# Queries and keys of eighteen couples loaded in 32-row quarters and turned by VectorE's block transpose

## The chip, the core and the metric

The kernel runs on one core of a Trainium2 chip. Its engines work from queues of their own and meet through semaphores: TensorE (PE in the profile; its weight loads are PEld), VectorE (DVE), ScalarE (ACT), GpSimd (POOL) and SyncE (SP), which here only issues DMAs. The metric is the device time of one execution in microseconds (us); the kernel before has a median of 1347.96 us over three runs.

## The reference

All data is float32. Attention over 8 batches of 12 heads with 448 rows of 64 is followed by a feed-forward block over the 3584 rows that come out.

```python
def rmsnorm(x, g):
    rms = np.sqrt(np.mean(x * x, axis=-1, keepdims=True) + 1e-06)
    return x / rms * g
q_n, k_n = (rmsnorm(q, g_q), rmsnorm(k, g_k))
scores = (1.0 / np.sqrt(64)) * np.matmul(q_n, k_n.transpose(0, 1, 3, 2))
scores = scores - np.max(scores, axis=-1, keepdims=True)
attn = np.exp(scores)
attn = attn / (np.sum(attn, axis=-1, keepdims=True) + 1e-09)
attn_out = np.matmul(attn, v)
# (B, H, S, D) -> (B * S, H * D), then
h = x @ w_in                          # 3584 x 768 by 768 x 2048
g = h * (1.0 / (1.0 + np.exp(-h)))
return g @ w_out                      # 2048 x 768
```

## The kernel before, in words

**Stages.** The 96 heads are worked off in 24 couples of four heads, `c` = 0 to 23 (two pairs, index `i`, of two heads, index `h`); three couples make a batch, and six (`GROUP`) two batches. Couples 0 to 5 run with little else beside them. From couple 6 on, the first product of the feed-forward block for the two batches before is worked in between, as a filler. After couple 23 come the first product of the last two batches and then the whole second product ("quads"). Both products save multiplications by sums of quarters (classes `Seven` and `deep`), whose additions are on VectorE and GpSimd. Everything in this stretch is recorded in an order that is written out by hand: each engine executes its instructions in just the order in which the loop `visit(c)`, `between(c)` issues them.

**A couple.** `visit(c)` makes scores of key tile by key tile on TensorE (`scores`, L595), exponentials on ScalarE (L600), and the weighted sums of `v` (`weigh`, L632). Scores are made transposed, with keys on partitions, so 1/rms of a key can be the scale of the exponential: `norm.column` is the `rms` operand at L600. A query's 1/rms has to be on its row before it is turned. Keys beyond 384 of the 448 are a tile of their own (`LEFT`). In the visit after, `weigh` finishes the couple and `divide` (L690) multiplies the two sums `av` by reciprocals. `turn` (L608) writes one column of a bank from ScalarE where the order of the two halves of `weigh` changes, which makes TensorE wait for the products so far.

**Between couples.** `transpose_q(c + 1)` turns the rows of q on TensorE, 8 transposes into PSUM (L558), and ScalarE copies them to `qT` (L562); `transpose_k` does the same for k with 7 (L576) and the copy applies the gains (L578). `sum_up` sums the exponentials on TensorE (L666), VectorE takes reciprocals (L675), and `spread` sends them to the partitions where `divide` needs them, by four and then two DMAs (L681, L683) on SyncE. `fill` issues the filler's products (L767) up to a share of columns: from couple 6 on about 14 steps (28 instructions) in each of its two calls. While it does so it deals out the work in `others` evenly, and the work in `prompt` one piece at the start and one after each third step. The results of the products leave their PSUM banks (`mm`, two of them) by VectorE (L725) or ScalarE (L775, L785), GpSimd adds parts (L787, L788), ScalarE applies SiLU in place (L905), and SyncE saves the hidden rows to DRAM (L800).

**Norms.** `normalise(c)` squares rows on ScalarE (L401), reduces them on VectorE (L402), forms mean + eps there (L426), takes the power -1/2 on GpSimd (L430), and, for q alone, multiplies the rows by it on GpSimd (L445). For q the columns are 16 of 112 partitions, for k 14 of 128.

**Loads.** All go through SyncE in program order: for one couple from 6 on q by 2 DMAs (L245), k by 4 (L252, L256), v by 1 (L261) and the last keys' v by 3 (L266, L269). Row `4p + j` of q lies on partition `p`, so the rows of `out` come out in that order, and `store` writes four interleaved pieces. From couple 6 q has one place (`q0`), k two. Until couple 8 W_in's pieces are loaded as well (L75), and until couple 10 they are rounded (L90, L91, L113, L116, L120, L124), and sums of them are made on VectorE (`sum_w_in`).

Of the kernel before, what the change touches and what calls it, by code (L numbers as in the profile page):

```python
# [30 lines left out]
class Shapes:  # L31
    def __init__(self, q, w_in):
# [19 lines left out]
        assert self.NW == self.NPAIR and self.B % 2 == 0  # L52

# [127 lines left out]
def kernel(  # L181
# [32 lines left out]
    ring = const.tile([P, nq + 2 * z.NK + nv + 2 * (4 * D + 2 * D)], F32, name="rows")  # L214
    place, at = {}, 0
    for name, size in (
        ("q0", nq), ("k0", z.NK), ("k1", z.NK), ("v", nv),
        ("vlast0", 4 * D), ("vlast1", 4 * D), ("vleft0", 2 * D), ("vleft1", 2 * D),
    ):
        place[name] = ring[:, ds(at, size)]  # L220
        at += size
# [10 lines left out]
    def load_q(c, t, by_head, steps=1):  # L232


        b, cp = divmod(c, z.NPAIR // 2)
        rows = q[b, ts(cp, 4)]
        if by_head:
            for i in range(steps):
                n = 4 // steps
                dst = t[0:R, ts(i, nq // steps)].rearrange("p (n j d) -> p n (j d)", n=n, j=J)  # L240
                nc.sync.dma_start(dst, rows[ts(i, n)].rearrange("n (p j) d -> p n (j d)", j=J))
            return
        for i in range(2):
            dst = t[0:R, ts(i, nq // 2)].rearrange("p (j h d) -> p j h d", j=J, h=2)
            nc.sync.dma_start(dst, rows[ts(i, 2)].rearrange("h (p j) d -> p j h d", j=J))  # L245

    def load_k(c):
        t = place[f"k{c % 2}"]
        main, left = keys_of(k, c)
# [7 lines left out]

    def load_v(c):
        main, _ = keys_of(v, c)
# [3 lines left out]
    def load_v_rest(c):  # L263
        main, left = keys_of(v, c)
# [22 lines left out]
    rms = [const.tile([P, 32], F32, name=f"rms{i}") for i in range(2)]  # L287
    spare = const.tile([P, 3 * J * D], F32, name="squares")
# [17 lines left out]
    with tc.manual_schedule(), tc.tile_pool(  # L306
        name="ps_first", bufs=1, space=bass.MemoryType.PSUM
    ) as ps_first:
        load_q(0, first_q, True, 2)
        load_k(0)  # L310
        load_q(1, second_q, True)
# [48 lines left out]
    def arm():  # L360
# [9 lines left out]
                second_q=second_q,  # L370
# [77 lines left out]
def store(nc, out, z, column, o, m0, *queues):  # L448
# [3 lines left out]
    while at < o.shape[0]:  # L452
        b, c = divmod(column + at, z.S)
        j, p = divmod(c, z.R)
# [8 lines left out]
def bounded(  # L463
# [10 lines left out]
    NC, loads, place, norm, spare, ones, first = (  # L474
        own[name] for name in ("NC", "loads", "place", "norm", "spare", "ones", "first")
# [52 lines left out]
    def load_q(c):  # L528

        if 0 < c < GROUP:  # L530
            loads["q"](c, raw_of(c), True)
        elif GROUP <= c < NC:
            loads["q"](c, q_of(c), False)
# [15 lines left out]
    def transpose_q(c):  # L549
# [13 lines left out]
        if c == GROUP - 2:  # L563
            load_q(GROUP)
        elif c >= GROUP:
            load_q(c + 1)

    def transpose_k(c):
# [10 lines left out]
        if c + 2 < NC:  # L579
            loads["k"](c + 2)  # L580

# [4 lines left out]
    def scores(c, j, i=None):  # L586
# [12 lines left out]
        for h in range(2):  # L599
            nc.scalar.activation(  # L600
                eleft[:, h] if j == LEFT else weights(c, j)[:, i, h], two[:, h, 0:S], AF.Exp,
                scale=norm.column(c, i, h, j),
            )

    def turn(step):

        if step != weighed["step"]:
            nc.scalar.copy(banks[1][:, S : S + 1], minus_half)  # L608
# [85 lines left out]
    def normalise(c):  # L694


        if c >= NC:
            return []

        def piece(name, i):  # L700
            t = scratch[i if c < GROUP + 2 else 0]
            source = raw_of(c) if c < GROUP else q_of(c)
            if name == "q":
                norm.squares_q(c, source, t, i)
            else:
                norm.squares_k(c, place[f"k{c % 2}"], t, i)
            if name == "q" and c < GROUP:
                norm.root(c, name, i)
                norm.scale(c, source, q_of(c), i, nc.gpsimd)
                if i == 1 and c + 2 < GROUP:  # L710
                    load_q(c + 2)
            elif i == 1:
                norm.root(c, name)
                if name == "q":
                    for m in range(2):
                        norm.scale(c, source, q_of(c), m, nc.gpsimd)
# [400 lines left out]
    def save_out(q, i, j):  # L1117
        for t in range(2):
            store(
                nc, out, z, (4 * q + 2 * (i - 1) + t) * P, results[i, j][t], (j - 1) * z.HALF,  # L1120
                nc.gpsimd if q == QUADS - 1 and i == 2 else nc.sync,
# [476 lines left out]
```

## Time and profile before

| | |
|---|---|
| runs | 1347.61, 1347.96, 1348.33 us; median 1347.96 |
| profiled execution | 1347.41 us, of which the span of the profile is 1345.6 |
| busy in the span | PE 1312.5 us (98%), DVE 915.4 (68%), ACT 519.6 (39%), POOL 346.3 (26%) |
| TensorE clock granted | 0.999 of full speed |
| DMA, from 160 to 733 us | 16 engines busy for 0.32, 89 GB/s |
| PE busy, 0 to 113 us | 102.5 of 113 |
| PE busy, 113 to 160 us | 42.9 of 47 |
| PE busy, 160 to 733 us | 563.4 of 573 |
| PE busy, 733 to 1346 us | 603.7 of 613 |

The stretch from 113 us is the hand-over from couple 5 to couples 6 and 7, that from 160 us holds couples 7 to 23, and that from 733 us what follows. An engine's busy time tells nothing of what waits for what; for that there is the chain that ended last, which follows each step back to what released it, and, behind a row of the timeline, the idle time before it with its releaser. A row `L430 POOL ... x23 | 64.2, 2791 | 143.5 <-DVE rms L426` reads: 23 instructions of line 430 on GpSimd, 64.2 us busy in all, 2791 ns each on the mean, 143.5 us of idle time of that engine just before them, ended most often by VectorE's line 426. `SPq` is the time in which SyncE's sequencer issues a DMA.

### The profile page before, as it was taken

To read this page: it belongs to the slowest core of one execution; us is meant where nothing else is said; L and a number is where in the kernel's file an instruction comes from. 1 tells how busy PE (TensorE), PEld (TensorE's weight loads), DVE (VectorE), ACT (ScalarE), POOL (GpSimd) and SP (SyncE) were. 2 spreads that over 40 slices of the span, in tenths; PEclk is the share of its full clock that TensorE was granted. 3 is DMA by queue.
4 is the path that set the end of the run, shared out by engine and by line. 5 is a ranking of instruction groups with operands and counts; after the bars stand their busy time and mean duration, and the time that the engine had idled before them with its cause. 6 is when DMAs were issued, how large, how long until landed. Compare 5 with 4: busy or idle time off the path is not lost.

```text
span 1345.6 us, 19745 instructions
## 1 busy us (share of the span) xinstructions
PE 1312.5 (98%) x7345; PEld 848.1 (63%) x7345; DVE 915.4 (68%) x1593; ACT 519.6 (39%) x932; POOL 346.3 (26%) x241
## 2 busy tenths in 40 slices
PE   8989999999999999999999999999999999999997
PEld 4333444444444444444444455557999999999997
DVE  5787776785645444644544586789878787878785
ACT  7866565655445455545544244320000000101000
POOL 6766534343133233332231044420000000000001
PEclk9999999999999999999999999999999999999999
DMA  8564437223223223222311257422323232322311
GB/s 234 161 166 113 124 89 203 76 80 106 74 81 80 79 78 101 74 72 80 106 52 38 100 175 262 150 98 68 104 75 99 75 100 79 99 92 88 115 59 39
DMA packets 175421, 139.41 MB, mean 104 GB/s; under 512 B 104052, under 2 KB 159284, under 8 KB 175316
## 3 DMA queue, kind: packets, MB, share of 16 engines
q1 hardware_dynamic: 174640, 137.08, 34.4%
q8 instruction: 60, 0.98, 0.3%
q0 software_dynamic: 352, 0.79, 0.2%
q14 instruction: 45, 0.37, 0.1%
q10 hardware_dynamic: 324, 0.20, 0.1%
HBM read 88.47 MB, written 41.29 MB: 96 GB/s over the span
## 4 chain that ended last, share of the span: by engine, by line
PE 83%; DVE 5%; ACT 5%; DMA 3%; issue 2%; SPq 1%; POOL 0%; ACTq 0%; DVEq 0%; POOLq 0%
PE mm L767 25%; PE alone L1074 22%; PE mm L1074 7%; PE av L632 7%; PE alone L767 7%; PE sc L595 7%; PE alone L1111 2%; DVE work L675 1%; PE sc L558 1%; DMA work<-work 1%; PE sc L576 1%; DMA hidden<-stage 1%; PE sc L666 1%; ACT work L600 1%; ACT L1358 1%
## 5 line engine op out<-in xcount | busy, mean ns | idle before, releaser
L767 PE MATMUL mm<-x,W 128*128 128x448 f32 x636 | 253.9, 543 | 3.1 <-DVE stage L725 1.2
L600 ACT ACTIVATE work<-sc,rms 128x448 f32<-128x448 f32 x324 | 184.9, 634 | 76.8 <-PE sc L595 63.9
L430 POOL TENSOR_TENSOR rms<-rms,minus_half 128x14 f32<-128x14 f32 (+4 forms) x55 | 140.9, 2563 | 236.5 <-DVE rms L426 187.0
L767 PEld LDWEIGHTS mm<-x,W 128*128 128x128 f32 x636 | 117.8, 190 | 125.0 <-issue 107.3
L767 PE MATMUL mm<-sums_x,W 128*128 128x448 f32 x456 | 183.0, 542 | 2.0 <-DVE parts L725 2.0
L632 PE MATMUL av<-work,rows 64*64 64x448 f32 x1296 | 156.1, 543 | 12.2 <-ACT av L608 9.6
L595 PE MATMUL sc<-work 64*64 64x448 f32 x1344 | 165.4, 542 | 1.1 <-ACT work L600 1.1
L646 DVE TENSOR_TENSOR work<-work 128x896 f32<-128x896 f32 (+1 forms) x114 | 124.5, 1125 | 49.2 <-PE av L632 48.6
L767 PEld LDWEIGHTS mm<-sums_x,W 128*128 128x128 f32 x456 | 85.3, 190 | 87.7 <-issue 80.8
L457 POOL DMA_DIRECT2D out_dram<-x x4 | 2.2, 565 | 442.7 <-DVE x L725 442.7
L632 PEld LDWEIGHTS av<-work,rows 64*64 64x64 f32 x1296 | 59.3, 132 | 86.3 <-issue 34.2
L595 PEld LDWEIGHTS sc<-work 64*64 64x64 f32 x1344 | 56.0, 132 | 75.8 <-issue 25.9
L402 DVE TENSOR_REDUCE rms<-squares 112x8 f32<-112x512 f32 (+1 forms) x80 | 52.2, 652 | 65.1 <-ACT squares L401 61.2
L1074 PE MATMUL alone<-W,rows 128*128 128x192 f32 x488 | 92.1, 326 | 0.0
L787 POOL TENSOR_TENSOR parts<-parts,stage 128x448 f32<-128x448 f32 x31 | 42.1, 1357 | 161.7 <-DVE parts L725 161.7
L1074 PEld LDWEIGHTS alone<-W,rows 128*128 128x128 f32 x488 | 81.5, 190 | 0.0
L1074 PE MATMUL alone<-W,work 128*128 128x192 f32 x382 | 72.2, 326 | 0.0
L905 ACT ACTIVATE stage<-stage 128x896 f32<-128x896 f32 x63 | 57.3, 945 | 26.1 <-DVE stage L725 25.4
L1084 ACT COPY squares<-alone 128x192 f32<-128x192 f32 x34 | 10.8, 317 | 137.5 <-PE alone L1074 79.0
L1074 PEld LDWEIGHTS alone<-W,work 128*128 128x128 f32 x382 | 63.8, 190 | 0.0
L401 ACT ACTIVATE squares<-rows 128x512 f32<-128x512 f32 (+1 forms) x74 | 44.8, 605 | 47.7 <-DVE rms L402 46.0
L675 DVE RECIPROCAL work<-sc 128x224 f32<-128x224 f32 x36 | 55.6, 1547 | 11.1 <-PE sc L666 11.1
(249 smaller groups left out, 2122.2 us busy)
## 6 DMA issues: line engine op xcount, KB each, us to landing
hidden<-stage SPq DMA_DIRECT2D x63, 448.0 KB, 2.7
work<-hidden SPq DMA_DIRECT2D x21, 1024.0 KB, 5.0
rows<-in_moe_w_out_dram SPq DMA_DIRECT2D x32, 384.0 KB, 3.4
W<-in_moe_w_in_dram SPq DMA_DIRECT2D x22, 512.0 KB, 5.1
rows<-in_k_dram SPq DMA_DIRECT2D x48, 192.0 KB, 3.1
work<-work SPq DMA_DIRECT2D x144, 56.0 KB, 1.9
rows<-in_q_dram SPq DMA_DIRECT2D x36, 224.0 KB, 3.5
x<-hidden SPq DMA_DIRECT2D x7, 1024.0 KB, 5.7
```

The lines of the kernel that those rows point to most:

```text
L401: nc.scalar.activation(t, rows, AF.Square)
L402: nc.vector.tensor_reduce(out=out, in_=t.rearrange("p (n d) -> p n d", n=n), axis=AX.X, op=ALU.add)
L430: nc.gpsimd.tensor_tensor(out=t, in0=t, in1=half, op=ALU.pow)
L595: nc.tensor.matmul(two[ds(half * D, D), h, 0:S], keys[rows, ts(half, D)], qT[rows, pair, :], start=True, stop=True,)
L600: nc.scalar.activation(eleft[:, h] if j == LEFT else weights(c, j)[:, i, h], two[:, h, 0:S], AF.Exp, scale=norm.column(c, i, h, j),)
L632: nc.tensor.matmul(sums[i][ds(h * D, D), :], v, w, start=(j == 0 and step == 1), stop=(j == LEFT - 1 and step == 1),)
L646: nc.vector.tensor_tensor(out=total, in0=total, in1=more, op=ALU.add)
L675: nc.vector.reciprocal(out=r[0][:, rows], in_=t[:, rows])
L767: nc.tensor.matmul(t, self.left(name, s), self.right(name, s), start=s == ends[0], stop=s == ends[1])
L787: nc.gpsimd.tensor_tensor(out=u2, in0=u2, in1=p5, op=ALU.add)
L905: nc.scalar.activation(t, t, AF.Silu)
L1074: nc.tensor.matmul(t, x[:, i], y, start=i == ORDER[0], stop=i == ORDER[-1])
```

## The change

For couples 6 to 23, q and k are loaded so that the 32x32 blocks of the tile are turned in place. A head's 448 rows are 14 blocks of 32 rows; the two halves of its 64 features go to two quarters of 32 partitions each, for two heads 128 partitions. In a row of the tile lie 14 blocks x 2 pairs of 32 values: 128 x 896. VectorE's block transpose then gives `qT` or `kT` at once, in SBUF, without PSUM and without the copy for q (`flip`); ScalarE still applies the gains, now in place.

Since a row's features lie in two quarters, each quarter gives half a sum of squares (`sum_squares`: one Square and one reduction for 128x896). One matmul with a matrix that has ones at its own and at the partner's place adds the halves (`pair_up` makes that matrix of `ident` once, after the last use as an identity); VectorE forms mean + eps of the result, and GpSimd takes the power and multiplies the rows, for k now too (`scale`). So the exponential gets the scale 1.0 in place of k's column. `scale` for couple `c + 2` stands at the end of `between(c)`; for couples 6 and 7 it has earlier or later places of its own.

Rows and keys are in plain order from couple 6 on, so v is loaded in plain order (4 DMAs for the first tiles, 4 for the last ones), and `store` writes rows of `out` from batch 2 on in one piece for each batch that a tile touches. The place `q0` has moved to the end of the ring and the squares share the end of it that the new q does not use. `turn(1)` uses VectorE in couples from 6 on. The four sums of one set of W_in's weights are dealt out in one fill in place of two. Couples 0 to 5 are as before.

```diff
@@ Shapes @@
+        self.Q = 32
+        assert 2 * self.S == self.NK and 4 * self.Q == self.P and self.D == 2 * self.Q
+
+    def quarters(self):
+
+        return [
+            (h, half, ds((2 * h + half) * self.Q, self.Q)) for h in range(2) for half in range(2)
+        ]
@@ loads @@
+    def load_quarters(rows, t):
+
+        rows = rows.rearrange("n (a p) d -> n p a d", p=z.Q)
+        for i in range(2):
+            for h, half, quarter in z.quarters():
+                dst = t[quarter, ts(i, z.S)].rearrange("p (a e) -> p a e", e=z.Q)
+                nc.sync.dma_start(dst, rows[2 * i + h][:, :, ts(half, z.Q)])
+
+    def load_q(c, t, steps=1):
 
 
         b, cp = divmod(c, z.NPAIR // 2)
         rows = q[b, ts(cp, 4)]
-        if by_head:
-            for i in range(steps):
-                n = 4 // steps
-                dst = t[0:R, ts(i, nq // steps)].rearrange("p (n j d) -> p n (j d)", n=n, j=J)
-                nc.sync.dma_start(dst, rows[ts(i, n)].rearrange("n (p j) d -> p n (j d)", j=J))
+        if c >= z.NPAIR:
+            load_quarters(rows, t)
             return
-        for i in range(2):
-            dst = t[0:R, ts(i, nq // 2)].rearrange("p (j h d) -> p j h d", j=J, h=2)
-            nc.sync.dma_start(dst, rows[ts(i, 2)].rearrange("h (p j) d -> p j h d", j=J))
+        for i in range(steps):
+            n = 4 // steps
+            dst = t[0:R, ts(i, nq // steps)].rearrange("p (n j d) -> p n (j d)", n=n, j=J)
+            nc.sync.dma_start(dst, rows[ts(i, n)].rearrange("n (p j) d -> p n (j d)", j=J))
 
     def load_k(c):
         t = place[f"k{c % 2}"]
+        if c >= z.NPAIR:
+            b, cp = divmod(c, z.NPAIR // 2)
+            load_quarters(k[b, ts(cp, 4)], t)
+            return
...
+    def plain_v(c, i):
+
+        b, cp = divmod(c, z.NPAIR // 2)
+        rows = v[b, ds(4 * cp + 2 * i, 2)]
+        start = i * z.LEFT
+        main = rows[:, ds(start, z.KEYS * P)].rearrange("h (j p) d -> p h j d", p=P)
+        return main, rows[:, ds((1 - i) * z.KEYS * P, z.LEFT)].rearrange("h p d -> p h d")
+
     def load_v(c):
+        if c >= z.NPAIR:
+            dst = place["v"].rearrange("p (i h j d) -> p i h j d", i=2, h=2, d=D)
+            for i in range(2):
+                for h in range(2):
+                    source = plain_v(c, i)[0][:, h, 0 : z.KEYS - 1]
+                    nc.sync.dma_start(dst[:, i, h], source)
+            return
...
     def load_v_rest(c):
+        if c >= z.NPAIR:
+            for i in range(2):
+                main, left = plain_v(c, i)
+                dst = place[f"vlast{c % 2}"][:, ts(i, 2 * D)]
+                nc.sync.dma_start(dst.rearrange("p (h d) -> p h d", h=2), main[:, :, z.KEYS - 1])
+                dst = place[f"vleft{c % 2}"][ds(i * z.LEFT, z.LEFT)]
+                nc.sync.dma_start(dst.rearrange("p (h d) -> p h d", h=2), left)
+            return
@@ squares and corrections have places of their own @@
-    rms = [const.tile([P, 32], F32, name=f"rms{i}") for i in range(2)]
-    spare = const.tile([P, 3 * J * D], F32, name="squares")
+    rms = [const.tile([P, 56], F32, name=f"rms{i}") for i in range(2)]
+    spare = rows[:, ds(at, 3 * J * D)]
+    squares = rows[:, ds(at - (nq - z.NK), z.NK)]
+    assert z.NK <= 3 * J * D + nq - z.NK
@@ store: rows of out in order from batch 2 on @@
+        if plain is not None and b >= plain:
+            n = min(z.S - c, o.shape[0] - at)
+            queues[0].dma_start(out[ds(b * z.S + c, n), ds(m0, o.shape[1])], o[ds(at, n), :])
+            queues = queues[1:] + queues[:1]
+            at += n
+            continue
@@ transposes @@
-        elif c >= GROUP:
-            load_q(c + 1)
 
     def transpose_k(c):
 
+    def flip(c, name):
+
+        if name == "q":
+            nc.vector.transpose(qT.rearrange("p i s -> p (i s)"), q_of(c)[:, 0 : z.NK])
+            load_q(c + 1)
+            return
+        nc.vector.transpose(kT, place[f"k{c % 2}"])
+        nc.scalar.activation(kT, kT, AF.Copy, scale=gains)
+        if c + 2 < NC:
+            loads["k"](c + 2)
+
+    n = z.NK // z.Q
+
+    def sum_squares(c, name):
+
+        if c >= NC:
+            return
+        rows = q_of(c)[:, 0 : z.NK] if name == "q" else place[f"k{c % 2}"]
+        nc.scalar.activation(squares, rows, AF.Square)
+        nc.vector.tensor_reduce(
+            out=norm.rms[c % 2][:, ts("qk".index(name), n)],
+            in_=squares.rearrange("p (n e) -> p n e", e=z.Q), axis=AX.X, op=ALU.add,
+        )
+
+    def scale(c, names="qk"):
+
+        if c >= NC:
+            return
+        start = "qk".index(names[0]) * n
+        f = norm.rms[c % 2][:, ds(start, len(names) * n)]
+        t = ps.tile([P, 2, BANK], F32, name="sc", bufs=2)[:, 0, 0 : len(names) * n]
+        nc.tensor.matmul(t, ident, f, start=True, stop=True)
+        nc.vector.tensor_scalar(
+            out=f, in0=t, scalar1=1.0 / D, scalar2=1e-6, op0=ALU.mult, op1=ALU.add
+        )
+        for i, name in enumerate(names):
+            rows = q_of(c)[:, 0 : z.NK] if name == "q" else place[f"k{c % 2}"]
+            rows = rows.rearrange("p (n e) -> p n e", e=z.Q)
+            factor = f[:, ts(i, n)]
+            nc.gpsimd.tensor_tensor(
+                out=factor, in0=factor, in1=minus_half.to_broadcast([P, n]), op=ALU.pow
+            )
+            factor = factor.rearrange("p (n one) -> p n one", one=1).to_broadcast([P, n, z.Q])
+            nc.gpsimd.tensor_tensor(out=rows, in0=rows, in1=factor, op=ALU.mult)
+
+    def pair_up():
+
+        for h, half, quarter in z.quarters():
+            other = ds((2 * h + 1 - half) * z.Q, z.Q)
+            nc.gpsimd.tensor_copy(ident[quarter, other], ident[quarter, quarter])
 
@@ scores, turn @@
-                scale=norm.column(c, i, h, j),
+                scale=norm.column(c, i, h, j) if c < GROUP else 1.0,
             )
 
-    def turn(step):
+    def turn(step, copy):
 
         if step != weighed["step"]:
-            nc.scalar.copy(banks[1][:, S : S + 1], minus_half)
+            copy(banks[1][:, S : S + 1], minus_half)
 
@@ visit @@
-        beside = normalise(c + 1) if c <= GROUP else []
+        if c < GROUP - 1:
+            beside = normalise(c + 1)
+        elif c <= GROUP:
+            beside = [lambda: sum_squares(c + 1, "q")]
+        else:
+            beside = []
         if c < NC:
...
-            turn(1)
+            turn(1, nc.scalar.copy if c < GROUP else nc.vector.tensor_copy)
...
+        if c == GROUP - 1:
+            scale(c + 1, "q")
         scores(c, 1, 0)
@@ sums of weights @@
-    sums_halves.update({8: [(3, 0), (3, 1)], 9: [(3, 2), (3, 3)]})
+    sums_halves[8] = [(3, step) for step in range(4)]
@@ between @@
+            if c == GROUP:
+                flip(c + 1, "q")
+            if c < GROUP - 1:
                 transpose_k(c + 1)
+            elif c < NC - 1:
+                flip(c + 1, "k")
...
+        elif c == GROUP:
+            scale(c + 1)
+        elif c < NC - 1:
+            flip(c + 1, "q")
...
-        further = normalise(c + 2) if c >= GROUP - 1 else []
-        fill(late + weights_in(c, 0) + further[2:])
+        keys = [lambda: sum_squares(c + 2, "k")] if c >= GROUP - 2 else []
+        queries = [lambda: sum_squares(c + 2, "q")] if c >= GROUP else []
+        fill(late + weights_in(c, 0) + keys)
         prompt = transposes_and_sums() if GROUP // 2 <= c != GROUP - 1 else []
         if c == GROUP // 2:
             begin(make_ahead([0, 1]), AHEAD * 2 * HW * S, GROUP - 1)
-        fill(weights_in(c, 1) + (further[:2] if c >= GROUP else []), prompt)
+        fill(weights_in(c, 1), prompt + queries)
+        if c == GROUP - 2:
+            pair_up()
+            scale(c + 2, "k")
+        elif c >= GROUP:
+            scale(c + 2)
```

## Prediction

> **What bounds the kernel now.** Couples (four heads each) are numbered as in the code, c = 0 to 23; the change touches c = 6 to 23. I read the page's slices first: PE is nine tenths busy or more in nearly every one. Then the chain of work that ended last, in the steady middle (start, length, what):
>
> ```profile
> 628.42 0.92 PE sc L558 x8
> 629.33 10.54 PE mm L767 x28
> 639.87 0.77 PE sc L576 x7
> 640.63 0.89 PE sc L666 x8
> 641.52 10.72 PE mm L767 x28
> 652.24 0.91 PE sc L595 x8
> ```
>
> Between two couples everything on the path is TensorE: turning q (L558), a first fill of products, turning k (L576), the sums, a second fill, the next scores. One couple takes 34.8 us, of which the turning is 0.92 + 0.77 = 1.69. From 160 to 733 us PE is idle for 9.6 us in all; 7.5 of that waits for ScalarE's one-column copy at L608.
>
> The hand-over from c = 5 to 6 is different. Its timeline (brackets give the idle time before, and its releaser):
>
> ```profile
> 113.86 0.60 PE L558 MATMUL sc<-ident,rows 112*128 112x112 f32 x4 [0.28 <-POOL rows L445]
> ...
> 120.98 2.47 SPq L681 DMA_DIRECT2D work<-work  x4
> ...
> 125.43 1.14 SPq L683 DMA_DIRECT2D work<-work  x2
> ...
> 128.00 1.21 DVE L690 TENSOR_TENSOR x<-av,work 128x448 f32<-128x448 f32 x2 [1.53 <-DMA work<-work]
> ...
> 128.68 1.18 PE L632 MATMUL av<-work,rows 64*64 64x448 f32 x6 [1.25 <-DVE x L690]
> ```
>
> Here the spread of the reciprocals over SyncE (L681, L683) gates VectorE's division, and that gates TensorE; from the spread's first issue to the division are 7.0 us. Last, GpSimd's groups by shape, for what will grow:
>
> ```profile
> L430 POOL TENSOR_TENSOR rms<-rms,minus_half 128x14 f32<-128x14 f32 x23 | 64.2, 2791 | 143.5 <-DVE rms L426 94.3 <-ACT work L578 49.0
> L430 POOL TENSOR_TENSOR rms<-rms,minus_half 112x16 f32<-112x16 f32 x18 | 52.5, 2918 | 84.5 <-DVE rms L426 84.5
> ...
> L445 POOL TENSOR_TENSOR rows<-rows,rms 112x512 f32<-112x512 f32 x36 | 41.2, 1164 | 1.4
> ...
> L430 POOL TENSOR_TENSOR rms<-rms,minus_half 128x6 f32<-128x6 f32 x1 | 1.3, 1311 | 0.0
> ```
>
> The power is priced by its columns: 1.31 us for 6, and undisturbed 2.58 for 14 and 2.90 for 16, so 0.16 a column on 0.36.
>
> [...] This trace has no block transpose; the reduction at L402 (674 ns for 512 columns, 552 for 384) shows about that rate, so 896 columns should take 1.05 us. [...] L445 is 1.04 us undisturbed and 1.46 beside L722. [...] In the trace an issue costs SyncE about 0.62 us for pieces of 32 or 64 partitions (L681, L256) and 0.39 for L261 with 128. [...] In the trace a q load of 1792 pieces of 256 B fills the 16 engines for about 2.3 us, 20 ns a piece.
>
> **The change, steady part (the 16 hand-overs c = 7 to 22).** Removed on the path: 1.69 each. Added on it: the matmul in the new `scale` that adds half sums across quarters (128x128 weights, 56 columns). Other f32 products run as two instructions with a weight load of 0.19 each; [...] 0.40, an estimate[...]. Net 1.29 x 16 = -20.5. It waits for a Square of q on ScalarE and a reduction on VectorE, asked for after 6 of the second fill's 14 steps: 6 us of cover for 1.0 + 1.05. Without that cover it costs up to 2 a couple.
>
> The first L608 copy of a visit moves from ScalarE, where it stood behind table loads and exponentials, to a VectorE that is idle then. Of the 7.5 us I take 5; the rest stays where the exponentials themselves are late.
>
> Off the path: VectorE gains two transposes (2.1) and trades four reductions (2.6) for two (2.1); it was busy 17 us of 35. ScalarE loses the 0.91 copy of qT and some squares. GpSimd's powers become two of 28 columns, 0.36 + 28 x 0.16 = 4.8 each (2.9 if the price stops growing[...]), and its products two of 128x896, 896/512 x 1.04 = 1.85. These four run in a row, 13.3 us, from the start of a visit of 11.9. The turned q needs the first two: hidden. k is needed 10 us later: hidden. L787 of the fills queues behind them; in one couple of three it comes 2.5 us into the first fill and is then slightly late: +1 in all.
>
> SyncE: q takes 8 issues in place of 2, k 8 in place of 4, v 8 in place of 4; with spread and saves some 20 us of 33. The q load ends 5.2 + 3 us after its transpose and has 15. k's issues end 6.5 us after the first fill; the spread follows, the division is possible at 13.5 and TensorE needs it at 15.9: hidden, by 2.4. In c = 8 SyncE also waits for two weight pieces whose rounding on GpSimd now stands behind the 13.3 us: it is some 4 us late, then the saves of hidden rows, then ScalarE's copies into the stage buffers: +4. In c = 10 VectorE does four sums of weights in one fill: +1. `out` is stored in fewer pieces; the end of the kernel is a VectorE chain, so 0.
>
> Steady sum: -20.5 - 5 + 1 + 4 + 1 = -19.5.
>
> **The start (c = 4 to 7)**, on the times above:
> 1. After c = 4, k's correction matmul waits until GpSimd, behind a weight rounding that ends at 103.6, has copied four blocks of `ident`: scores(5) at 105.1, not 101.8.
> 2. GpSimd's 13.3 us run from 105.4 to 118.7. q is turned by 119.8, k by 120.8.
> 3. 16 issues at 0.65 now stand ahead of the spread: it starts at 129.9, not 121.0; division at 136.9, not 128.0. TensorE is 8.9 late there.
> 4. The sums of x follow on VectorE; TensorE's first fill begins 7.5 late (no turning of q).
> 5. Couple 7's correction stands behind those sums on VectorE, so GpSimd scales from 148.4 to 161.7. L787 waits for that; VectorE stands at the third product until 163.4, both banks stay full, and TensorE's next product starts 12.1 late.
> 6. Behind it on VectorE stand a reduction, two transposes and a reciprocal, 4.7: the next bank is 15.1 late.
> 7. The load of q for couple 8 followed that transpose: issued to 170.8, landed about 173.3, Square until 174.3, and ScalarE's copy of a product stands behind it: 16.5 late.
> 8. k's issues end at 176, so the division falls at 183; the weighing in visit 7 starts at 183.7, before at 165.5: 18.2 late.
>
> Sum: 18.2 - 19.5 = -1.3, against the profiled execution's 1347.41 us (1345.6 of span, 1.8 around it), which lies 0.55 below the median shown. So about 1347: the start eats what 16 couples save.
>
> **Rivals.**
> Faster, 1339: the power's price stops growing with the columns. At 2.9 the four take 9.5: step 5 ends 4 earlier and carries 6 to 8 with it, c = 8 loses 2 less, L787 is never late. Together -8. It decides from about 4.2 us a power. The three sizes in the trace speak against it, but none has over 16 columns.
> Slower, 1364: the ring of small pieces becomes the bound. A quarter is 448 pieces of 128 B, 0.028 us of 16 engines per ns of a piece; at 20 ns 0.56, just inside an issue's 0.65. At 36 ns eight take 8.1 in place of 5.2, 0.5 more than the cover of 2.4; in 16 couples and twice in the start, +15 with q. It decides from some 33 ns. [...] against: the DMA share is 0.32 from 160 to 733.
> Slower, 1355: a block transpose takes twice my price. The start has four on its path (+4), and the couple of three with a late reciprocal loses 1 each (+4).
> That the change does not do what it says is no rival: in the changed program the TensorE rows of these turnings are gone and 36 block transposes stand on VectorE.
>
> **How the numbers follow.** Forecast 0.42, with its own range 1340 to 1355 (steps 5 to 8 hang on one another, each estimate moves them by 2); faster rival 0.28; the ring 0.15; the transpose 0.10; anything else 0.05, slower. A measurement of this kernel can tell about 0.2%, 2.7 us. The forecast gives 0.12 faster, 0.20 same, 0.10 slower; the faster rival 0.25 and 0.03; the transpose 0.01 same; all else is slower: 0.37, 0.24, 0.39. A tenth cut at each end: 1335 to 1364.
>
> **What would show it.** Right: 33.5 us per steady couple with PE's waits near 3 in sum; powers near 4.8, issues near 0.65; TensorE gaps before the divisions near 137 and 183, and L787 late near 162. Wrong: the start's gaps small, or a wait of PE on DVE or ACT that recurs in every couple.

## The result, and the profile after

The changed kernel takes 1369.36 us (median of four runs, 1367.72 to 1371.07) where the kernel before takes 1347.78 beside it: 1.0161 times the time before, 95% interval 1.0144 to 1.0179. The forecast was 1347.0 with a range of 1335 to 1364; the time lies above it. The profiled execution took 1367.72 us with a span of 1365.9, against 1345.6 before: 20.3 us to be found.

The chain of work that ended last, in a steady couple of the changed kernel (start, length, what):

```profile
607.02 0.91 PE sc L695 x8
...
617.73 10.72 PE mm L858 x28
628.45 1.19 PE sc L766 x8
629.63 2.47 PE mm L858 x6
...
637.63 0.62 DVE stage L816
638.25 0.04 issue
638.30 4.03 PE mm L858 x10
642.32 0.16 PE sc L662 x2
642.48 0.91 PE sc L695 x8
```

The two turnings are gone from between the products, as foreseen, and the matmul of `scale` (L662) has 0.16 us of the chain. This is the worst couple of three, 35.5 us long, with a merge of VectorE (L816) in the chain; the other two take 34.3 and 33.6. Over couples 11 to 22 the mean is 34.3, where 35.4 were taken before; the 34.8 from which the prediction started was one couple, and not the mean.

The timeline of the hand-over from couple 5 to couple 6 in the changed kernel answers to the one shown of before:

```profile
124.98 4.07 SPq L249 DMA_DIRECT2D rows<-in_k_dram  x8
129.48 2.73 SPq L781 DMA_DIRECT2D work<-work  x4
132.95 1.24 SPq L783 DMA_DIRECT2D work<-work  x2
...
135.69 1.21 DVE L790 TENSOR_TENSOR x<-av,work 128x448 f32<-128x448 f32 x2 [4.00 <-DMA work<-work]
...
136.37 1.18 PE L732 MATMUL av<-work,rows 64*64 64x448 f32 x6 [2.13 <-DVE x L790]
```

The spread begins at 129.48, behind the quarter loads, and the division falls at 135.69, 7.7 us later than before. GpSimd's groups by shape in the changed kernel:

```profile
L670 POOL TENSOR_TENSOR rms<-rms,minus_half 128x28 f32<-128x28 f32 x36 | 176.3, 4896 | 96.5 <-DVE rms L663 96.5
L674 POOL TENSOR_TENSOR rows<-rows,rms 128x896 f32<-128x896 f32 x36 | 64.4, 1790 | 2.8
```

A power of 28 columns takes 4.90 us and a product 1.79: the four of a couple take 13.4.

**Where the 20.3 us are.** A useful mark for this is the division (L690 before, L790 after) in each visit. The table, worked out from timelines of the profiled executions, gives how many microseconds later it starts than in the kernel before (minus: earlier); the last column is the difference of the spans. Visit 8 divides what couple 7 has weighed, so that a step from visit 8 to visit 9 is what couple 8 lost. A profiled execution can differ from its kernel's median, by 3.3 us in the kernel begun at 12 and by some 2 at most in the others, and the rows start with 0.1 to 1.8 us at the first division, where couples 0 to 5 still run as before: the steps along a row tell more than its level. The rows below the first belong to the experiments.

| kernel | visit 8 | 9 | 10 | 11 | 23 | span |
|---|---|---|---|---|---|---|
| changed | 16.1 | 24.9 | 27.6 | 34.3 | 21.2 | 20.3 |
| changed, weights' loads on another queue | 17.8 | 19.0 | 21.7 | 27.2 | 14.1 | 15.0 |
| begun at 9 | 3.0 | 11.3 | 14.0 | 20.7 | 8.6 | 9.0 |
| begun at 9, loads on another queue | 2.6 | 3.2 | 4.9 | 11.6 | -0.7 | 1.6 |
| begun at 12 | 1.4 | 0.9 | -0.6 | 7.0 | -5.7 | -3.3 |
| begun at 12, early pairs | 0.7 | 0.2 | -1.3 | 1.3 | -11.4 | -11.0 |
| before, with powers | 1.2 | 9.3 | 9.3 | 11.6 | 17.3 | 17.0 |

In the changed kernel three stretches stand out: the start loses 16.1 up to visit 8; couples 8, 9 and 10, while W_in is still being rounded, lose 8.8, 2.7 and 6.7, 18.2 in all; the twelve couples 11 to 22 win 13.1. The start had been forecast at 18.2; the middle had been put at about nothing.

Couple 8 holds the longest single gap of TensorE. Its timeline in the changed kernel:

```profile
210.67 4.80 POOL L670 TENSOR_TENSOR rms<-rms,minus_half 128x28 f32<-128x28 f32 x1 [1.47 <-DVE rms L663]
...
222.37 1.70 POOL L674 TENSOR_TENSOR rows<-rows,rms 128x896 f32<-128x896 f32 x1
...
224.03 4.24 POOL L133 TENSOR_TENSOR W<-W 128x512 int32<-128x512 int32 x2
226.19 0.35 SPq L84 DMA_DIRECT2D W<-in_moe_w_in_dram  x1
228.29 0.35 SPq L84 DMA_DIRECT2D W<-in_moe_w_in_dram  x1
...
234.81 4.20 SPq L249 DMA_DIRECT2D rows<-in_q_dram  x8
239.11 1.05 SPq L891 DMA_DIRECT2D hidden<-stage  x2
...
241.95 0.53 ACT L876 COPY stage<-mm 128x448 f32<-128x448 f32 x1 [10.95 <-DMA hidden<-stage]
...
242.53 4.85 PE L858 MATMUL mm<-x,W 128*128 128x448 f32 x6 [7.88 <-ACT stage L876]
```

Read from the bottom: TensorE waits 7.88 us for a bank that ScalarE has not copied out; ScalarE has waited 10.95 for the save of the stage buffer; the save stands on SyncE behind q's eight quarter loads, the loads of v and the weights' loads (L84); those wait for the rounding (L133) on GpSimd; and the rounding stands behind the powers and products that began at 210.67. In the kernel before, the same save and copy are these:

```profile
206.63 0.43 SPq L75 DMA_DIRECT2D x<-in_moe_w_in_dram  x1
211.82 1.61 SPq L800 DMA_DIRECT2D hidden<-stage  x2
217.14 0.53 ACT L785 COPY stage<-mm 128x448 f32<-128x448 f32 x1 [4.69 <-DMA hidden<-stage]
```

ScalarE waits 4.69 us for the save there too, but the copy is still in time for TensorE: there is hardly any slack left. Counted from the 16.1 us that visit 8 is late, the save in the changed kernel is 11.2 us later than before: 6.0 of them had built up when the last of the weights' loads was issued (228.69 against 206.63), and 5.2 are added because sixteen loads stand between it and the save, where six stood.

### The profile page after: what moved, and what is told of

It reads as the page before. It is cut to its first block, busy times and chain, and to the rows that moved or that the text cites. A ratio compares the mean times of both kernels' runs of the same rounds, so it can differ in the third digit from the quotient of the medians.

```text
span 1365.9 us, 19539 instructions
## 1 busy us (share of the span) xinstructions
PE 1301.1 (95%) x7113; PEld 818.2 (60%) x7113; DVE 956.5 (70%) x1595; ACT 476.3 (35%) x859; POOL 445.5 (33%) x241
## 4 chain that ended last, share of the span: by engine, by line
PE 80%; DVE 7%; issue 4%; ACT 3%; DMA 2%; POOL 2%; SPq 1%; ACTq 0%; DVEq 0%; POOLq 0%
PE mm L858 23%; PE alone L1165 22%; PE sc L695 8%; PE av L732 8%; PE mm L1165 7%; PE alone L858 7%; PE alone L1202 2%; DVE work L746 2%; DVE work L775 1%; PE sc L766 1%; SPq L249 1%; ACT stage L996 1%; POOL rms L670 1%; PE mm L1202 1%; DVE rms L650 1%
## 5 line engine op out<-in xcount | busy, mean ns | idle before, releaser
L858 PE MATMUL mm<-x,W 128*128 128x448 f32 x636 | 262.7, 556 | 23.4 <-ACT stage L876 11.1
L670 POOL TENSOR_TENSOR rms<-rms,minus_half 128x28 f32<-128x28 f32 x36 | 176.3, 4896 | 96.5 <-DVE rms L663 96.5
L746 DVE TENSOR_TENSOR work<-work 128x896 f32<-128x896 f32 (+1 forms) x114 | 138.8, 1242 | 46.6 <-PE av L732 46.1
L732 PE MATMUL av<-work,rows 64*64 64x448 f32 x1296 | 148.6, 539 | 8.3 <-DVE x L790 2.7
L700 ACT ACTIVATE work<-sc 128x448 f32<-128x448 f32 x252 | 120.9, 542 | 97.4 <-PE sc L695 85.4
L1165 PE MATMUL alone<-W,rows 128*128 128x192 f32 x608 | 113.0, 326 | 0.0
L878 POOL TENSOR_TENSOR parts<-parts,stage 128x448 f32<-128x448 f32 x31 | 42.0, 1356 | 209.8 <-DVE parts L816 209.8
L1165 PEld LDWEIGHTS alone<-W,rows 128*128 128x128 f32 x608 | 101.2, 190 | 0.0
L650 DVE TENSOR_REDUCE rms<-rows 128x28 f32<-128x896 f32 x36 | 38.7, 1076 | 44.3 <-ACT rows L649 44.2
L674 POOL TENSOR_TENSOR rows<-rows,rms 128x896 f32<-128x896 f32 x36 | 64.4, 1790 | 2.8
L1175 ACT COPY rows<-alone 128x192 f32<-128x192 f32 x34 | 10.8, 318 | 136.9 <-PE alone L1165 78.7
```

What stands on the lines that cost most here:

```text
L650: nc.vector.tensor_reduce(out=norm.rms[c % 2][:, ts("qk".index(name), n)], in_=squares.rearrange("p (n e) -> p n e", e=z.Q), axis=AX.X, op ...
L670: nc.gpsimd.tensor_tensor(out=factor, in0=factor, in1=minus_half.to_broadcast([P, n]), op=ALU.pow)
L674: nc.gpsimd.tensor_tensor(out=rows, in0=rows, in1=factor, op=ALU.mult)
L700: nc.scalar.activation(eleft[:, h] if j == LEFT else weights(c, j)[:, i, h], two[:, h, 0:S], AF.Exp, scale=norm.column(c, i, h, j) if c < ...
L732: nc.tensor.matmul(sums[i][ds(h * D, D), :], v, w, start=(j == 0 and step == 1), stop=(j == LEFT - 1 and step == 1),)
L746: nc.vector.tensor_tensor(out=total, in0=total, in1=more, op=ALU.add)
```

## Experiments

**Begun at couple 12.** Theory A: the loss sits in the start and in the rounding couples. Both are gone when couples 6 to 11 keep TensorE's transposes. The identity's pairs and the first `scale` then come at the end of couple 10. In the same way from 9 on, with the pairs at the end of couple 7. In all kernels that begin later, `turn(1)` is VectorE's from couple 6 on, as in the change. The four sums of weights stay in one fill in those from 9; in those from 12 three are in the first fill and one in the second.

```diff
-        if c >= z.NPAIR:            # in load_q, load_k, load_v, load_v_rest
+        if c >= z.START:
             load_quarters(rows, t)
...
-        if c < GROUP - 1:
+        if c + 1 < z.START:
             transpose_q(c + 1)
...
+        if c + 2 == z.START:
+            pair_up()
+        if c + 2 >= z.START:
+            scale(c + 2)
```

> The same path of rows, quarters and block transposes, begun at couple 12 instead of 6; couples 6 to 11 keep TensorE's transposes. Theory A (the loss of the change sits in the start, +15 us up to visit 7, and in couples 8 to 11, +18 us, where weights are rounded behind GpSimd's powers and products; each later couple gains about 1.15 us): 1347.8 - 12 x 1.15 = 1334 us, 1331 to 1337. Theory B (the path of rows has a start-up cost wherever it is begun, some +15 us): 1347.8 + 15 - 9 = 1354 us or more. Theory C (16 loads of q and k a couple on SyncE's queue delay the saves and so TensorE): C has to hold in couples 12 to 22 too, so no gain: 1346 us or more.

> The same, begun at couple 9: the start of couples 4 to 7 is as before the change, the weights' rounding in couples 8 and 10 still stands behind GpSimd's chain. Theory A: only the start's share is given back: 1369.4 - 15 = 1354 us, 1349 to 1358, with TensorE's long gap in couple 8. Theory B: about what it costs from 6 on, less three couples' gain: 1366 us or more.

Measured: from 12, 1340.84 us (ratio 0.9939, 0.9921 to 0.9956); from 9, 1356.99 (1.0067, 1.0050 to 1.0083). From 9 came out within A's interval: going from 6 to 9 gives 12.4 us, and couple 8's gap is still there (8.3 us lost between visits 8 and 9). From 12 was faster than before, so B and C fall, but A's 1334 was missed by 6.8 us, and its interval by 3.8. The table shows the loss in couple 10, 7.6 us between visits 10 and 11. This is the place, in the timeline of the kernel from 12:

```profile
300.74 0.99 POOL L688 COPY ident<-ident 32x32 f32<-32x32 f32 x4
301.78 0.67 PE L670 MATMUL sc<-rms,ident 128*128 128x56 f32 x2 [2.27 <-POOL ident L688]
302.38 1.77 PE L703 MATMUL sc<-work 64*64 64x448 f32 x8
...
303.93 3.21 PE L740 MATMUL av<-work,rows 64*64 64x448 f32 x16
```

TensorE waits 2.27 us for the four small copies of `pair_up`, which stand behind two sums on GpSimd, and then runs slowly: eight score products take 1.77 us (0.98 elsewhere), sixteen weighing products 3.21 (1.68).

**The pairs made early.** GpSimd has nothing to do after the last key transpose of couple 11.

```diff
                 transpose_k(c + 1)
+                if c + 2 == z.START:
+                    pair_up()
...
-        if c + 2 == z.START:
-            pair_up()
```

> The kernel of the first experiment with one thing moved: the four small copies that pair the quarters in the identity are issued on GpSimd right after the last key transpose of couple 11 and not at that couple's end. Theory A (the 7.6 us that the first experiment loses between visits 10 and 11 is TensorE's 2.3 us wait for these copies and the slower matmuls after it): 1340.8 - 5 = 1336 us, 1334 to 1338. Rival (beginning the path costs this by itself): 1339 us or more.

Measured: 1336.84 us, 0.9924 (0.9910 to 0.9937), as A had it. The intervals of this ratio and of that without the early pairs overlap; what the profile adds is that the wait of 2.27 us is gone and that couple 10 loses 2.6 us in place of 7.6. This is the fastest version found, and it beats both kernels. From visit 11 to visit 23 it wins 12.7 us in twelve couples, 1.06 in each.

**What holds couple 8.** Three runs go at the chain read above. The first does it to the kernel before, with nothing but two unused powers:

```diff
+        if GROUP <= c < NC - 2:
+            for _ in range(2):
+                nc.gpsimd.tensor_tensor(out=idle_power, in0=idle_power,
+                    in1=minus_half.to_broadcast([P, 28]), op=ALU.pow)
```

> The kernel before, with nothing of the change but two idle powers of 128x28 on GpSimd (9.8 us, their result unused) at the end of couples 6 to 21. Theory A: couple 8's saves wait behind the rounding as in the changed kernel; +6 to +14 us: 1354 to 1362 us. Theory C: within 2 us of before.

Measured: 1365.06 us, 1.0126 (1.0108 to 1.0144). Two idle powers a couple make the kernel before almost as slow as the change did. Couple 8 alone loses 8.0 us, by the same chain (timeline of that kernel; here L124 rounds, L75 loads weights, L800 saves, L785 is ScalarE's copy):

```profile
211.73 3.38 POOL L124 TENSOR_TENSOR W<-W 128x512 int32<-128x512 int32 x2
213.04 2.43 SPq L75 DMA_DIRECT2D W<-in_moe_w_in_dram  x2
...
221.38 1.44 SPq L800 DMA_DIRECT2D hidden<-stage  x2
...
226.09 0.53 ACT L785 COPY stage<-mm 128x448 f32<-128x448 f32 x1 [8.12 <-DMA hidden<-stage]
...
226.68 4.85 PE L767 MATMUL mm<-x,W 128*128 128x448 f32 x6 [6.95 <-ACT stage L785]
```

The save is 8.4 us later in its couple than in the kernel before, although q has only two loads there. The total was above A's interval, since A had left out a second effect: in couples 10, 14, 17 and 20 another 1.9 to 2.4 us each are lost, in the last three while VectorE's merges, which follow GpSimd's two sums of a half block, are late for TensorE by 0.95 and 0.39 us.

The second run changes the order on GpSimd: k's power and product stand after the roundings of visits 8 and 10.

```diff
+        elif c + 1 in visits:
+            scale(c + 2, "q")
         elif c >= GROUP:
             scale(c + 2)
@@ weights_in_visit @@
+        if c in visits:
+            scale(c + 1, "k")
```

> The changed kernel, but in couples 7 and 9 only q's power and product are issued at the end of the couple; k's stand after the two roundings of weights in the next visit. Theory A: the roundings of visit 8 end 6.7 us earlier, the weights' loads and the saves behind them on SyncE's queue too, and the 7.9 us gap of TensorE in couple 8 falls to 1 or 2 us: 1369.4 - 8 = 1361 us, 1358 to 1364. Theory C: SyncE's quarter loads delay the saves, and the order on GpSimd makes no difference: 1367 us or more.

Measured: 1370.85 us, 1.0164 (1.0144 to 1.0184): by its time a miss for A. In its profile the long gap is gone: the place shows 0.92 and 2.40 us, and couple 8 loses 4.9 us instead of 8.8. But k's correction now stands in the middle of visits and brings waits of its own, the longest in visit 10:

```profile
303.62 1.52 PE L695 MATMUL sc<-work 64*64 64x448 f32 x8 [2.34 <-DVE rms L663]
```

Scores wait for a bank that VectorE, busy with rounding, has not read; couple 10 loses 10.4 us instead of 6.7, and couple 9 4.3 instead of 2.7. The rest of the difference, 3.3 us, was there at visit 8 already, before the orders part. The run moved two things at once and doesn't decide.

The third run cuts the chain at SyncE. The weights' loads are issued on GpSimd's own queue, right behind the roundings that they wait for; saves no longer stand behind them.

```diff
-            self.nc.sync.dma_start(raw.bitcast(I64), src)
+            self.queue.dma_start(raw.bitcast(I64), src)   # nc.gpsimd from couple 7 on
```

> The changed kernel, but from couple 7 on the loads of the weights to be rounded are issued on GpSimd's queue, behind the rounding that they wait for anyway, and no longer on SyncE's, where the saves of hidden stand behind them. Theory A (in couple 8 GpSimd's 13.3 us delay the rounding, the rounding the weights' load, the load everything behind it on SyncE's queue, and the late save TensorE): the 7.9 us gap of couple 8 falls under 2 us, 1369.4 - 8 = 1361 us, 1358 to 1364. Theory C (the 8 loads of q's quarters that stand before the save are enough): the gap stays above 4 us, 1365 us or more.

> The path begun at couple 9, with the pairs made right after the last key transpose and the weights' loads on GpSimd's queue. Theory A: 1357 - 2 (pairs) - 8 (couple 8) = 1347 us, 1344 to 1350; what is still lost is in couples 9 and 10, where merges on VectorE stand behind rounding, turns and sums. Theory C: 1352 us or more.

Measured: 1363.12 us (1.0114, 1.0092 to 1.0136) for the first and 1347.03 (0.9986, 0.9976 to 0.9997) for the second, both within A's intervals. Couple 8 now loses 1.1 and 0.6 us. The waits there, in the changed kernel with the loads moved:

```profile
234.91 0.53 ACT L877 COPY stage<-mm 128x448 f32<-128x448 f32 x1 [0.48 <-DMA hidden<-stage]
```

GpSimd's chain was as long as ever, and q's eight loads still stand ahead of the save (SyncE issues them from 224.69, the save at 228.76, 10.4 us earlier than in the changed kernel). So theory C falls as a cause by itself: the price of couple 8 was the weights' load at the head of SyncE's queue, with the loads behind it making the delay longer. The second kernel also has the pairs early, so its gain of 10.0 over the kernel from 9 holds both.

**Couples 9 and 10.** They still lose 1.7 and 6.7 us in the kernel from 9 with the loads moved. One run takes couple 10's change alone, the four sums of weights in one fill, to the kernel before; one moves a Square and its reduction in couple 9.

```diff
-    sums_halves.update({8: [(3, 0), (3, 1)], 9: [(3, 2), (3, 3)]})
+    sums_halves[8] = [(3, step) for step in range(4)]
```

> The kernel before, with only the four sums of weights in the first fill of couple 10 and none in the second. My step charged 1 us: 1348 to 1349 us. Rival (these sums hold VectorE's merges of banks and make the 5 us loss of couple 10): 1352 us or more.

```diff
+        if c == GROUP + 3:
+            others = weights_in(c, 1)
+            fill(others[:2] + queries + others[2:], prompt)
```

> The kernel begun at couple 9 with the weights' loads on GpSimd's queue, and in couple 9 alone the Square and reduction of couple 11's q are dealt out after that fill's first opening and rounding of weights, in place of after three steps. Theory Q (TensorE's 3.0 us gap in couple 9 comes from the reduction, which waits 3 us for its Square on ScalarE behind SiLU, with the rounding and the merge of a bank behind it on VectorE): couple 9 loses 0 to 1 us in place of 2.5 to 3, 1344.5 us. Rival (the rounding alone makes the merge late): 1347 us as without it.

Measured: the sums 1349.30 us, 1.0009 (1.0003 to 1.0016), the 1 us that the step had charged. The Square moved: 1346.02, 0.9984 (0.9977 to 0.9990), 1.0 less than without it by the medians, while the intervals of the two ratios overlap; the time lies between what theory and rival had expected. TensorE's gap in couple 9 in the kernel from 9 with the loads moved, and then with the Square moved as well:

```profile
267.50 1.77 PE L873 MATMUL mm<-sums_x,W 128*128 128x448 f32 x4 [3.00 <-DVE stage L831]
```

```profile
266.09 1.77 PE L873 MATMUL mm<-sums_x,W 128*128 128x448 f32 x4 [1.50 <-DVE stage L831]
```

Half of the gap was the reduction that waits for its Square, and couple 9 loses nothing any more; the other half stays, with the rounding still ahead of the merge on VectorE. For couple 10 the trace of the changed kernel gives this:

```profile
304.22 1.70 POOL L674 TENSOR_TENSOR rows<-rows,rms 128x896 f32<-128x896 f32 x1
...
304.70 4.25 DVE L746 TENSOR_TENSOR work<-work 128x896 f32<-128x896 f32 x2
...
305.87 4.22 POOL L133 TENSOR_TENSOR W<-W 128x512 int32<-128x512 int32 x2
...
320.09 1.04 ACT L638 ACTIVATE work<-work,gains 128x896 f32<-128x896 f32 x1 [14.86 <-DVE work L637]
...
321.04 0.51 ACT L866 COPY stage<-mm 128x448 f32<-128x448 f32 x1
...
321.61 6.47 PE L858 MATMUL mm<-sums_x,W 128*128 128x448 f32 x12 [2.05 <-ACT stage L866]
```

VectorE's additions and GpSimd's rounding take 2.1 us each beside one another, where alone they take 1.04 and 1.29; the turn of k comes late behind the four sums; ScalarE, whose next instruction is the gain of the turned k, waits 14.86 us for it with the copy of a bank behind; TensorE waits for the copy. Its twelve products then take 6.47 us in place of 4.78, with a granted clock of 0.50 from 322.6 to 326.0. Two other waits of TensorE in this couple, 1.22 and 1.63 us, are for merges on VectorE. Here the sums cost more than in the kernel before, where ScalarE does not wait for VectorE's turn. This reading of couple 10 was not tried by a run of its own: its 6 to 7 us are argued, not shown.

**The turn copy, and the steady couples.** First the kernel before with only `turn(1)` on VectorE, then two changes to the kernel from 12 with early pairs: two sums from GpSimd to VectorE, and the gain of k from ScalarE to VectorE.

```diff
-            turn(1)
+            turn(1, nc.scalar.copy if c < GROUP else nc.vector.tensor_copy)
```

> The kernel before, with only the one-column turn copy of couples 6 to 24 on VectorE in place of ScalarE. My step: TensorE's waits for that copy go, 1347.8 - 5.5 = 1342 us. Rival (the wait moves to VectorE's own queue or to the next fill): 1347 to 1349 us.

```diff
-            nc.gpsimd.tensor_tensor(out=u2, in0=u2, in1=p5, op=ALU.add)
-            nc.gpsimd.tensor_tensor(out=done[2, 2], in0=u3, in1=p5, op=ALU.add)
+            adder.tensor_tensor(out=u2, in0=u2, in1=p5, op=ALU.add)   # nc.vector from couple 11 on
+            adder.tensor_tensor(out=done[2, 2], in0=u3, in1=p5, op=ALU.add)
```

> The same, and from couple 11 on the two sums of a half block that GpSimd makes (u2 + p5 and u3 + p5) are VectorE's. Theory P (in one couple of three they stand behind a power or product, worth 1.9 us in the powers-only experiment): 1336 - 7 = 1329 us. Rival (VectorE is as late with them, in its own order): within 2 us of the kernel with the early pairs, or slower.

```diff
-        nc.scalar.activation(kT, kT, AF.Copy, scale=gains)
+        nc.vector.tensor_scalar(out=kT, in0=kT, scalar1=gains, scalar2=None, op0=ALU.mult)
```

> Begun at couple 12 with early pairs, and the multiplication of the turned keys by the gains is VectorE's in place of ScalarE's. Theory S (ScalarE, whose queue waits up to 7.7 us for the turn of the keys, is what still holds up TensorE in the steady couples, 0.7 us in each): 1336.8 - 5 = 1332 us. Rival (VectorE is the tighter of the two, and 1 us more a couple delays its merges): 1337 us or more.

Measured: the turn alone 1346.70 us, 0.9994 (0.9986 to 1.0002), no difference that can be told; from visit 11 to visit 23 TensorE's idle time falls from 6.2 us to 2.5. The profiled execution of this run is 4.8 us ahead at visit 19 and gives most of it back, with a wait of TensorE for VectorE's copy of 0.98 us in visit 20 and of 1.54 in the last visit. The two sums 1340.46 (0.9947, 0.9933 to 0.9961) and the gain 1338.97 (0.9928, 0.9912 to 0.9945): both rivals were right: neither is faster than the kernel with the early pairs, and the gain's time can't be told from it. From 300 to 745 us TensorE's waits in the kernel from 12 with early pairs are two groups and a small one, the first of these fences; with the sums on VectorE they are the second:

```profile
PE mm L872 <- DVE stage L830: 4.7, 8, 0.8
PE mm L872 <- ACT stage L890: 2.0, 3, 0.7
PE mm L872 <- DVE parts L830: 0.8, 1, 0.8
```

```profile
PE mm L874 <- DVE stage L830: 5.3, 9, 0.8
PE mm L874 <- ACT stage L892: 2.0, 3, 0.7
PE mm L874 <- ACT stage L882: 1.9, 3, 0.6
PE mm L874 <- DVE parts L830: 0.8, 1, 0.8
```

Neither move lowers these waits in sum: 7.5 us with the early pairs, 10.0 with the sums on VectorE, and 11.4 with the gain there. Of the 7.5, 5.5 are waits for VectorE. That its own order is what holds up the steady couples is the likely reading; no run rearranged it.

## Why the prediction was wrong, step by step

**The start, steps 1 to 8: right in the main.** Scores of couple 5 began at 105.4 (said: 105.1). GpSimd's four ran from 105.9 to 119.7 (105.4 to 118.7), q was turned by 120.9 (119.8), the spread began at 129.5 (129.9), the division fell at 135.7 (136.9). Couple 7 was scaled from 145.9 to 160.4 (148.4 to 161.7), L878, as L787 is now called, followed at 160.4, and TensorE went on at 162.2 after a gap of 6.71. The second division was at 180.3 (183). Eight steps that hang on one another gave 18.2; 16.1 were measured at the next division. Part of the closeness is luck: an issue took 0.5 us and not 0.65, couple 7's correction began 2.5 us early but took 14.5 us and not 13.3, and three stretches in which the granted clock was 0.50 (last section) were in no step. Begun at couple 9, 13 of these 16 are gone at visit 8.

**The steady sum, the term "+4" for couple 8 and "+1" for couple 10: this failed.** The place and the chain in couple 8 were named rightly, GpSimd's 13.3 us, the weight pieces, the saves, ScalarE's copies. What failed is the step "it is some 4 us late". With the gain of 1.5 to 1.6 a couple that the same sum expects, couple 8 should have lost 2.4, and it lost 8.8. I let SyncE be 4 us late and stopped there: the weights' loads were 6.0 us late, and what follows in that queue was not added up. After the last of them at 228.69 stand eight loads of v and eight of q, and the saves come at 239.11, 11.2 us late. Then TensorE stood idle for 7.88 us, and its next six products took 4.85 us in place of 2.52, a cost that no step had. Couple 9 was not named at all (2.7, beside the gain not made), and in couple 10 I priced the four sums by themselves. By themselves they do cost 1 us; with the new turn behind them and ScalarE behind the turn the couple lost 6.7. Together couples 8 to 10 lost 18.2 us where the sum had them at about nothing: this is nearly all of the 22 us by which the forecast missed.

**"-20.5", the turnings less the correction: nearly right.** (1.29 x 16 is 20.6.) From visit 11 to visit 23 TensorE's busy time falls from 418.3 us to 403.7, 1.21 a couple where 1.29 were forecast. **"-5" for the turn copy: this failed too.** In the same twelve couples TensorE's idle time was to fall, and it rose from 6.2 us to 7.6: the waits for the turn copy are gone, but 7.5 us of waits for VectorE's merges and ScalarE's copies have come in their place. Moved alone, the turn copy gives 1.5 us by the medians, which can't be told from nothing. **"+1" for L787 late in one couple of three: too small.** The powers alone cost 1.9 us in such a couple, and the changed kernel has waits of 0.66, 0.78 and 0.67 us in every three couples. Over couples 11 to 22 these errors make 13.1 out of some 18 expected, 5 of the missing us; the start gave 2 back.

**The rivals.** The faster one falls: a power is 4.90 us, so its price grows with the columns as estimated (4.84). The ring falls: the loads of quarters are issued at 0.50 us each (I had taken 0.65) and land 2.2 us after issue, and the DMA share from 160 to 733 us is 0.36. The dear transpose falls: 1.10 us, where my estimate was 1.05. The time ended near the ring's 1364 for a reason that was no rival. A rival "a weight load holds SyncE's queue and the saves behind it" should have been one, with the point from which it decides: the slack that the stage buffers leave, which ScalarE's wait of 4.69 us for the save in the kernel before shows to be used up.

The sign that I had named for being wrong, a wait of PE that recurs in every couple, came only in part: the waits just named recur in every three couples. Most of the loss is in a few large gaps, and a sum made per couple and multiplied by 16 does not see them.

## What to carry to other kernels

When work is put on an engine that is off the path, list what shares its queue and, for each instruction that comes later, follow the wait through every queue where something stands behind it: here 10 us of GpSimd became 8 us of TensorE by way of a load at the head of SyncE's queue. Do it for each phase apart; a change that wins 1.06 us in a steady couple lost 34 where start-up and rounding shared the engines, and the same path begun after these phases is 11 us faster than the kernel before. A load that waits for an engine was better off on that engine's own queue than ahead of the saves: 6.2 us by the medians of the changed kernel.

## What the runs showed of the hardware

Around some gaps of TensorE the granted clock was 0.50 for some microseconds. Windows of the changed kernel around couple 8's gap (the engines' busy times, and after POOL's the granted clock, DMA share and GB/s):

```profile
234.00:242.50 8.50, 0.65 (x2) 0.00 (x0) 0.00 (x0) 0.55 (x2) 0.08 (x1) 0.69 0.73 181
242.50:247.40 4.90, 4.85 (x6) 1.85 (x6) 4.04 (x5) 2.73 (x4) 0.00 (x0) 0.50 0.78 242
247.40:252.00 4.60, 4.55 (x12) 2.42 (x13) 4.53 (x7) 1.10 (x2) 2.24 (x2) 0.98 0.57 101
```

The granted clock is 0.50 for the first 4.9 us after the gap, in which six products take 4.85 us, and back at 0.98 after. The length of a single gap does not decide here: after 2.27 us in the kernel from 12 eight score products took 1.77 us and sixteen weighing products 3.21 (0.98 and 1.68 elsewhere), while after 3.00 us in couple 9 of the changed kernel four products took 1.77 us with a granted clock of 1.00. The wait of 2.27 us thus cost its length and at least 2.3 us more (0.79 and 1.53 for these two groups). The mean granted clock of that profiled execution is 0.992; with the early pairs, which remove the wait, it is 0.998.

In the changed kernel it is 0.989, against 0.999 in the kernel before. Its trace has a clock of 0.50 in five stretches besides the very end, from 100.8, 124.7, 158.8, 237.3 and 322.6 us, 27.3 us in all, in which TensorE is busy for 18.2; the trace of before has none but at the very end. If that work took twice its time, as the six products above nearly did, the five cost TensorE up to 9 us, an estimate. Not all of it lengthens the kernel: six products from 123.42 took 3.65 us in place of 2.52, and TensorE waited for the division at 135.69 all the same. In couples 8 and 10 the slow products cost 2.3 and 1.7 us behind the gaps.

In couple 10 of the changed kernel two roundings on GpSimd and two additions on VectorE ran beside one another and took 2.1 us each, where alone they take 1.29 and 1.04. Beside GpSimd's powers VectorE's additions kept their time: two within the power that began at 299.18 in that couple took 2.09 together. The powers took 4.78 to 5.62 us, and the longest, from 145.90, ran beside four such additions; what slowed it was not tried.
